# Top-k attention and two MLPs on one core: other planner costs, and PSUM accumulators moved beside the scores

## The chip, the cores and the metric

The kernel runs on one core of a Trainium2 chip. The metric is the device time of one execution in microseconds (us); lower is better. TensorE (PE) does the matmuls, VectorE (DVE), ScalarE (ACT) and GpSimd (POOL) the element-wise work, and SyncE (SP) issues nearly all DMAs.

## The reference

Three stages follow each other on 2304 tokens of width 512 (4 batches of 576 tokens, 8 heads of 64):

```python
scores = scale * np.matmul(q, k.transpose(0, 1, 3, 2))
kth = np.partition(scores, -top_k, axis=-1)[..., -top_k:-top_k + 1]
scores = np.where(scores >= kth, scores, -1000000000.0)
attn = np.exp(scores - np.max(scores, axis=-1, keepdims=True))
attn = attn / (np.sum(attn, axis=-1, keepdims=True) + 1e-09)
x = np.matmul(attn, v)                       # top_k = 32 of 576 keys
h = x @ w_in                                 # first MLP, 512 -> 2048 -> 512
x = np.where(h >= 1, h, np.where(h <= -1, 0.0, (h + 1) ** 2 / 4)) @ w_out
h = np.maximum(x @ w_in, 0.0)                # second MLP, weights of its own
out = h * h @ w_out
```

Inputs and output are float32.

## The kernel before, in words

**Tiles.** The tokens are 18 tiles `T` of 128 rows. Attention goes by slots `t = 8 * T + j`, 144 in all, one for a tile and a head. Float32 values are split into a high and a low float16 part, so that a float32 product is three float16 matmuls (`mlp_in`, line 1044, and `mlp_out`, line 1097) or comes from pairs of parts laid side by side (`scores`, line 820, and `attend`, line 900).

**One slot.** `scores` writes 128x576 scores into PSUM with four matmuls (`both<-kst,qT` in the profile). `topk_ops` (line 835) finds the 32nd largest of each row on DVE: four MAX8 (eight largest each) with three MATCH_REPLACE8 between them that blank what was found; the first MAX8 and the first MATCH_REPLACE8 read PSUM (`m<-both`, `W<-m,both`), the rest the SBUF copy `W`. POOL makes two biases `nb` from the result (line 851). ACT reads the scores again (`below`, line 862, `W<-both,nb`), takes the exponential (line 868) and writes the high part (`pc<-W`, line 876); POOL subtracts to get the low part (line 885); a DMA transposes (`pT<-pc`, line 892); and `attend` sums the 14 products with the values and a column of ones into a 65-wide accumulator in PSUM (`acc<-vst,pT`).

**One tile.** `x_part` (line 940) runs twice a tile, for four slots each: DVE reads the sums in column 64 (`rs<-acc`), takes the reciprocal, and ACT, or DVE in tiles 4 and 13 (`x<-acc,rs`), scales the four accumulators into `x`. `x` is split and transposed to `T_x`. An MLP group is 12 matmuls in (`h<-wall,T_x` or `h<-wall,T_y`), an activation on ACT and DVE (`r`), a split (`g`), a transpose (`gT<-g`) and 12 matmuls out (`o<-wall,gT`); each tile has four groups in each MLP, and the second MLP runs a tile behind the first. In the first 250 us the weights are loaded and decoded too (`wall`, line 483: ACT, POOL and DVE in turn).

**PSUM.** One tile `both` (line 818) holds two score areas, columns 0 to 575 for even slots and 960 to 1535 for odd ones. One tile `acc` (line 898) holds seven accumulators used in turn. Two tiles each are for `h` and `o`. In the built program, instructions of different engines that touch one PSUM tile wait for each other in program order, also where they touch different columns of it and where both only read.

**What sets the order.** Nothing is issued when it is called. `Book.note` (line 185) records every instruction with what it depends on and a key (`PLAN`, line 35, gives each step an offset in units of an eighth of a slot). `Book.order` (line 279) is a list scheduler: it keeps a clock for each engine, takes the engine that can start first, and there the ready instruction with the lowest key. `Book.costs` (line 251) gives each instruction a time for which its engine is busy and a time until its result can be used. `Book.emit` (line 353) issues all in the planned order, so that each engine runs its own part in order; hence nearly all instructions of the profile have the line of `emit`, 356. In this planner two engines never exclude each other: only data, buffers and the engine's own queue set a start.

Of the kernel before, what the change touches and what calls it, by code (L numbers as in the profile page):

```python
# [8 lines left out]
F32 = mybir.dt.float32  # L9
# [7 lines left out]
P = 128  # L17
# [109 lines left out]
class Room:  # L127
    def __init__(self, ring, shape, dtype, name):
        self.ring, self.shape, self.dtype, self.name = ring, shape, dtype, name
        self.writes, self.reads, self.ends, self.first, self.left, self.end, self.at = [], [], [], None, 0, 0.0, None  # L130
# [13 lines left out]
class Op:  # L144
    __slots__ = ("n", "engine", "fn", "args", "kwargs", "deps", "succ", "tiles", "new", "cost", "key", "ready", "start", "missing", "load", "move")


class Book:
# [36 lines left out]
    def note(self, engine, method, fn, args, kwargs):  # L185
# [41 lines left out]

        if method == "matmul":
            p0, p1, at = outs[0].cover()[:3]
            ends = outs[0].tile.ends  # L230
            if kwargs["start"]:
                deps.update(n for a, b, bank, n in ends if bank == at // 2048 and a < p1 and p0 < b)
            if kwargs["stop"]:
                ends[:] = [e for e in ends if e[:3] != (p0, p1, at // 2048)] + [(p0, p1, at // 2048, op.n)]
# [10 lines left out]
        op.deps = deps  # L245
        op.cost = self.costs(engine, method, args, kwargs, outs, ins)
# [4 lines left out]
    def costs(self, engine, method, args, kwargs, outs, ins):  # L251
        n = outs[0].elements() if outs else 0
        if engine == "PE":
            a = args[1].tile.dtype
            c = max(n * (4 if a is F32 else 1) / 2370.0, 0.03)
            return c, c + 0.2
        both = sum(not v.tile.ring.psum for v in ins if v.elements() > 64)
# [7 lines left out]
        if engine == "ACT" and method == "dma_start_transpose":  # L265
            return 1.35, 5.0
# [3 lines left out]
        if engine == "POOL":  # L270
            c = 0.2 + n / 490 if method == "tensor_tensor" else 0.27 + n / 1050
            return c, c + 0.06
        if method == "dma_start":
            src = args[1]
            size = 4 * (n or args[1].elements()) * 128
            return 0.5, size / 1000 / 390
        return 1.32, n * 256 / 1000 / 165

    def order(self):
# [13 lines left out]
        out = []  # L293

# [15 lines left out]
        while len(out) < len(ops):  # L310
# [16 lines left out]
            op = ops[heapq.heappop(now[e])[1]]  # L327
            op.start = t
            busy, took = op.cost
            free[e] = t + busy  # L330
            if e == "SP":
                wire = max(wire, t + 1.6) + took
                end = wire + 0.3
# [35 lines left out]
def tile_topk_attention_mlp_mlp(  # L369
# [18 lines left out]
    def rings(name, bufs, **space):  # L388
# [4 lines left out]
    ps_s, ps_a, ps_h, ps_o = (  # L393
        rings(n, m, **psum) for n, m in (("ps_s", 1), ("ps_a", 1), ("ps_h", 2), ("ps_o", 2))
    )
# [422 lines left out]
    both = ps_s.tile([P, 1536], F32, tag="s", name="both")  # L818

    def scores(t):  # L820
# [3 lines left out]
        d["s"] = ps = both[:, 960 * odd : 960 * odd + S]  # L824
# [115 lines left out]
    def x_part(T, half):  # L940
# [4 lines left out]
        runs = []  # L945
# [445 lines left out]
```

## Time and profile before

| | us |
|---|---|
| three timed executions | 1137.35, 1132.17, 1139.06 |
| median of them | 1137.35 |
| span of the profiled execution, first to last instruction | 1130.8 |
| median less that span | 6.55 |
| PE busy in it | 988.4 |
| DVE busy in it | 925.7 |
| ACT busy in it | 861.7 |
| POOL busy in it | 715.5 |

The page gives no other time for the profiled execution than its span, so what lies around the span is taken as those 6.55 us. "Busy" is the time in which at least one instruction of an engine runs. A matmul's record lasts longer than the distance to the next one, since matmuls are pipelined. A wait is shown as "engine and what it was to write <- engine and what that wrote last", with its total, the number of times, and the longest.

### The profile page before, as it was taken

The numbers are of one execution on the slowest core, as the hardware profiler recorded it, in microseconds if no ns is written. First come the engines' busy times: TensorE is split into PE (matmuls) and PEld (weight loads), VectorE is DVE, ScalarE is ACT, GpSimd is POOL, SyncE is SP. The second block draws the span as 40 slices with busy tenths as digits, with TensorE's granted clock in tenths as the row PEclk, the third lists the DMA queues.
The fourth block names the chain that finished last, engine by engine and source line by source line (L and its number), as shares of the span: only waits on it lengthen the run. The fifth ranks groups of instructions, "written<-read, shape, count | busy, mean of one in ns | idle before, by whom it ended". The sixth has DMA issues, their size and how long they took to land. (4 is left out here: it accounts for less than half of the span.)

```text
span 1130.8 us, 20675 instructions
## 1 busy us (share of the span) xinstructions
PE 988.4 (87%) x6676; PEld 479.8 (42%) x6676; DVE 925.7 (82%) x1967; ACT 861.7 (76%) x1605; POOL 715.5 (63%) x1182
## 2 busy tenths in 40 slices
PE   1267776688899999999999999999999999999997
PEld 1033333234344444444444444444444444444443
DVE  5899987798899898998989898998889998983100
ACT  4778989799768787878888777878777778776443
POOL 4696989889676755657775655567775646453221
PEclk9569887789999999999999999999999999999999
DMA  7989878667788666868877667778867676564332
GB/s 227 313 283 253 215 175 196 133 140 139 145 146 153 113 122 115 163 120 156 158 156 137 118 122 123 150 136 161 155 120 131 123 127 108 109 117 88 75 66 56
DMA packets 463389, 165.22 MB, mean 146 GB/s; under 512 B 441776, under 2 KB 448944, under 8 KB 463280
## 3 DMA queue, kind: packets, MB, share of 16 engines
q1 hardware_dynamic: 459856, 163.05, 70.2%
q10 hardware_dynamic: 3424, 0.85, 0.4%
q8 instruction: 52, 0.85, 0.3%
q14 instruction: 57, 0.47, 0.2%
HBM read 55.31 MB, written 4.72 MB: 53 GB/s over the span
## 5 line engine op out<-in xcount | busy, mean ns | idle before, releaser
L356 PE MATMUL o<-wall,gT 128*128 128x512 f16 x1728 | 420.1, 382 | 19.7 <-DMA gT<-g 19.2
L356 DVE MAX8 m<-W 128x8 f32<-128x576 f32 x432 | 326.6, 758 | 8.4
L356 POOL TENSOR_TENSOR g<-r,g 128x512 f16<-128x512 f32 x144 | 168.2, 1168 | 147.3 <-ACT g L356 124.4
L356 POOL TENSOR_TENSOR pc<-W,pc 128x64 f16<-128x64 f32 (+1 forms) x288 | 207.3, 740 | 84.2 <-ACT pc L356 65.4
L356 PEld LDWEIGHTS <-gT 128*128 128x128 f16 x1728 | 163.9, 98 | 222.8 <-DMA gT<-g 34.2
L356 PE MATMUL h<-wall,T_x 128*128 128x512 f16 x864 | 213.3, 390 | 8.5 <-DVE r L356 8.2
L356 DVE MATCH_REPLACE8 W<-m,W 128x576 f32<-128x576 f32 x288 | 213.8, 742 | 0.0
L356 PE MATMUL h<-wall,T_y 128*128 128x512 f16 x864 | 208.8, 380 | 1.3 <-DVE r L356 1.1
L356 ACT ACTIVATE W<-both,nb 128x576 f32<-128x576 f32 x144 | 106.3, 739 | 87.0 <-DVE W L356 32.5
L356 DVE MAX8 m<-both 128x8 f32<-128x576 f32 x144 | 108.9, 757 | 36.7 <-PE both L356 13.3
L356 PE MATMUL both<-kst,qT 128*128 128x64 f16 (+3 forms) x640 | 101.8, 299 | 42.0 <-ACT W L356 33.8
L356 ACT ACTIVATE W<-W,nb,esc 128x576 f32<-128x576 f32 x144 | 124.1, 862 | 6.8 <-POOL nb L356 2.7
L356 PEld LDWEIGHTS <-T_x 128*128 128x128 f16 x864 | 83.0, 100 | 102.7 <-issue 18.3
L356 PEld LDWEIGHTS <-T_y 128*128 128x128 f16 x864 | 81.5, 98 | 92.3 <-issue 2.3
L356 PEld LDWEIGHTS <-pT 128*128 128x128 f16 (+1 forms) x2240 | 92.1, 101 | 51.0 <-issue 14.2
L356 ACT ACTIVATE g<-r 128x512 f16<-128x512 f32 x144 | 90.2, 626 | 24.1 <-DVE r L356 22.7
L356 DVE MATCH_REPLACE8 W<-m,both 128x576 f32<-128x576 f32 x144 | 107.6, 748 | 0.0
L356 PE MATMUL acc<-vst,pT 128*128 128x65 f16 (+1 forms) x2240 | 100.8, 196 | 4.5 <-DMA pT<-pc 3.8
L356 ACT ACTIVATE pc<-W 128x576 f16<-128x576 f32 x144 | 97.3, 676 | 0.9
L356 ACT ACTIVATE r<-r 128x512 f32<-128x512 f32 x144 | 90.1, 626 | 1.6
L356 POOL TENSOR_SCALAR nb<-m 128x1 f32<-128x1 f32 x144 | 31.1, 216 | 87.8 <-DVE m L356 76.1
L356 ACT ACTIVATE r<-h 128x512 f32<-128x512 f32 x72 | 42.5, 591 | 49.6 <-PE h L356 46.7
(143 smaller groups left out, 1130.0 us busy)
## 6 DMA issues: line engine op xcount, KB each, us to landing
wall<-in_moe_w_in_dram SPq DMA_DIRECT2D x32, 512.0 KB, 7.1
wall<-in_moe_w_out_dram SPq DMA_DIRECT2D x30, 512.0 KB, 5.2
out_dram<-ob SPq DMA_DIRECT2D x18, 256.0 KB, 2.5
l_q<-in_q_dram SPq DMA_DIRECT2D x16, 256.0 KB, 3.4
n_v<-in_v_dram SPq DMA_DIRECT2D x24, 144.0 KB, 2.8
n_k<-in_k_dram SPq DMA_DIRECT2D x12, 288.0 KB, 3.1
l_k<-in_k_dram SPq DMA_DIRECT2D x12, 288.0 KB, 3.3
pT<-pc SPq DMA_TRANSPOSE x144, 3.3
```

Source lines behind the costliest of these rows:

```text
L356: op.fn(*(real(a) for a in op.args), **{k: real(a) for k, a in op.kwargs.items()})
```

## The change

The planner's costs are new throughout (ACT, POOL, DVE, DMA, and 0.16 us instead of 0.2 us from a matmul to its user). Three exclusions are new in `order`: an instruction isn't started while another engine still holds a PSUM tile that it touches (`held`, `apart`); POOL and a DVE instruction with two large SBUF operands exclude each other in the same way (`"port"`); and an accumulation isn't opened while another is open in the same 2 KB and half of the rows of a tile (`taken`, `shut`), which replaces the dependence through `ends`. `PLAN` stays.

The PSUM layout changes too: two tiles `s0` and `s1` of two banks each (the profile and the order name both `s`, or `s0` and `s1`). Even slots have their scores in `s0`, odd ones in `s1`; the accumulators of even slots lie in `s1` and those of odd slots in `s0`, six in each. `attend` uses accumulator `t // 2 % 6` of its side, and `x_part` reads two accumulators on each side instead of a run of up to four.

```diff
         op.deps = deps
+        op.banks = {v.tile for v in views if v.tile.ring.psum}
+        if engine == "POOL" or engine == "DVE" and sum(not v.tile.ring.psum for v in ins if v.elements() > 64) > 1:
+            op.banks.add("port")
...
         if engine == "DVE":
-            if method in ("max", "match_replace"):
-                n = 576
-            if method == "tensor_scalar" and not any(v.tile.ring.psum for v in ins + outs):
-                n *= 0.8
-            c = 0.06 + n / 960 + (0.07 if method == "match_replace" else 0.25 if both > 1 else 0.06 if method != "max" else 0)
-            return c, c + 0.03
...
+            if method == "max":
+                return 0.68, 0.75
+            if method == "match_replace":
+                return 0.76, 0.85
+            c = 0.07 + (n if method != "tensor_reduce" else 128) / 960 + (0.05 if n > 64 else 0.0)
+            return c, c + 0.08
         if engine == "ACT":
-            c = 0.17 + n / 1400 + 0.1 * sum(isinstance(kwargs.get(k), View) for k in ("bias", "scale", "accum_out"))
-            return c, c + 0.12
...
+            c = 0.155 + n / 1400 - (0.03 if wide else 0.0) + 0.09 * aps - (0.04 if n < 300 else 0.0)
+            return c, c + 0.1
...
+        held, taken, shut = {}, set(), []
+
+        def apart(op, t):
+
+            return max([t] + [end for b in op.banks for e, end in held.get(b, {}).items() if e != op.engine])
...
             op = ops[heapq.heappop(now[e])[1]]
+            if not taken.isdisjoint(op.opens):
+                shut.append(op)
+                free[e] = t
+                continue
+            later = apart(op, t)
+            if later > t:
+                heapq.heappush(soon[e], (later, op.n))
+                free[e] = t
+                continue
...
+            for b in op.banks:
+                held.setdefault(b, {})[e] = t + took + 0.08
             free[e] = t + busy
-            if e == "SP":
+            if op.load:
                 wire = max(wire, t + 1.6) + took
-                end = wire + 0.3
+                end = wire + 0.7
+            elif op.move == "dma_start_transpose":
+                wire = max(wire, t + 1.1) + took
+                end = wire + 0.4
...
-    both = ps_s.tile([P, 1536], F32, tag="s", name="both")
+    pair = tuple(ps_s.tile([P, 1024], F32, tag=f"s{i}", name=f"s{i}") for i in range(2))
+    AREA = (pair[0][:, 0:S], pair[1][:, 1024 - S : 1024])
+    ACC = tuple(pair[1 - i][:, a : a + 6 * D1].rearrange("p (i d) -> p i d", d=D1) for i, a in enumerate((0, S)))
...
-        d["s"] = ps = both[:, 960 * odd : 960 * odd + S]
+        d["s"] = ps = AREA[odd]
...
-    acc = ps_a.tile([P, 7 * D1], F32, tag="a", name="acc").rearrange("p (i d) -> p i d", d=D1)
...
-                    acc[r0 : r0 + rn, t % 7, :],
+                    ACC[odd][r0 : r0 + rn, t // 2 % 6, :],
...
-            for j, n, i in runs:
-                DVE.tensor_scalar(rs[:, j : j + n], acc[:, i : i + n, D], 1e-9, None, op0=ALU.add)
+            for a in range(2):
+                DVE.tensor_scalar(pairs[:, a], ACC[a][:, i0 : i0 + 2, D], 1e-9, None, op0=ALU.add)
```

In the built program each engine has the same instructions as before, but for DVE: 72 instead of 51 additions `rs`, and 16 instead of 12 products `x` for tiles 4 and 13. SP has 373 transposes and 235 loads or stores in both. What moves is shown at three places around slots 79 to 81. Names carry the program's buffer numbers; `m8_79` is the maxima of slot 79, `W_79` its scores, `pT_77` the transposed probabilities of slot 77. A wait names the counter of the engine or DMA queue that is waited for.

On ACT, at the second reading of slot 79's scores (`W_79` from `both` or `s1`), before:

```order
L356 ACTIVATE ob_6_7383<-o_2_6_7069,z_6_6870 128x512 [waits PE_49]
L356 ACTIVATE W_79_7268<-both_193,nb_79_7356 128x576 [waits DVE_49,PE_49,Pool_49]
L356 ACTIVATE r_66_7394<-h_66_7335,B1_705,A1_753 128x512 [waits PE_49]
L356 ACTIVATE g_65_7404<-r_65_7345 128x512 [waits DMAHW5_49,DVE_49]
L356 ACTIVATE W_79_7268<-W_79_7268,nb_79_7356,esc_9_6221 128x576 [waits Activation_49,Pool_49]
```

and now:

```order
L383 ACTIVATE h_65_7296<-h_65_7296,NG_811,A2_789 128x512
L383 ACTIVATE W_79_7277<-s1_207,nb_79_7378 128x576 [waits PE_49,Pool_49]
L383 ACTIVATE W_79_7277<-W_79_7277,nb_79_7378,esc_9_6240 128x576 [waits Activation_49,Pool_49]
L383 ACTIVATE g_65_7397<-r_65_7336 128x512 [waits DMAHW0_49,DVE_49]
L383 ACTIVATE pc_79_7402<-W_79_7277 128x576 [waits DMAHW7_49,Activation_49]
```

The wait for DVE is gone here. Over the whole program the readings of scores on ACT that wait for a DVE instruction on the same PSUM tile go from 104 to 15 of 144.

On PE, from the last matmul of slot 81's scores to slot 77's sums over the values, before:

```order
L356 LDWEIGHTS qT_10_0_7116
L356 MATMUL both_193<-kst_2_0_6114,qT_10_0_7116 128x512
L356 LDWEIGHTS pT_77_7283 [waits DMAHW3_49]
L356 MATMUL acc_476<-vst_2_5_7180,pT_77_7283 128x65 [waits Pool_49]
L356 LDWEIGHTS pT_77_7283 [waits DVE_49]
```

and now:

```order
L383 LDWEIGHTS qT_10_0_6983
L383 MATMUL s1_207<-kst_2_0_6083,qT_10_0_6983 128x512
L383 LDWEIGHTS pT_77_7298 [waits DMAHW3_49]
L383 MATMUL s0_201<-vst_2_5_6975,pT_77_7298 128x65 [waits DVE_49]
L383 LDWEIGHTS pT_77_7298
```

The first of the 14 products now waits for a DVE counter: for slot 80's first MATCH_REPLACE8, which reads the scores in the same tile. Over the whole program the sums of 79 of the 144 slots wait so for DVE's reading of scores and 31 for ACT's, from slot 48 on 53 and 26 of 96; before, none did, and 34 waited for `rs` or `x` (as 10 do now). The scores of 41 slots waited for DVE's reading of the slot just before; none does now, and 45 wait for `rs` or `x`.

On DVE, the chain of slot 79 from its first MAX8 on, before:

```order
L356 MAX m8_79_7244<-both_193 128x8 [waits PE_49,Activation_49]
L356 MAX m8_78_7149<-W_78_7174 128x8 [waits DVE_49]
L356 MATCH_REPLACE W_79_7268<-m8_79_7244,both_193 128x576 [waits DVE_49,Pool_49]
L356 TENSOR_SCALAR rs_9_7276<-acc_476 128x4 [waits PE_49]
L356 SCALAR_TENSOR_TENSOR r_64_7228<-h_64_7188,G_731,r_64_7228 128x512 [waits Activation_49]
L356 RECIPROCAL rs_9_7276<-rs_9_7276 128x4 [waits DVE_49]
L356 MAX m8_79_7244<-W_79_7268 128x8
L356 MATCH_REPLACE W_79_7268<-m8_79_7244,W_79_7268 128x576 [waits DVE_49]
```

and now:

```order
L383 MAX m8_79_7269<-s1_207 128x8 [waits PE_49,Pool_49]
L383 MATCH_REPLACE W_79_7277<-m8_79_7269,s1_207 128x576 [waits DVE_49]
L383 SCALAR_TENSOR_TENSOR r_64_7246<-h_64_7197,G_778,r_64_7246 128x512 [waits Activation_49,Pool_49]
L383 TENSOR_SCALAR rs_9_7214<-s0_201 128x2 [waits PE_49,Activation_49]
L383 MAX m8_79_7269<-W_79_7277 128x8 [waits DVE_49]
L383 RECIPROCAL rs_9_7214<-rs_9_7214 128x4 [waits DVE_49]
L383 MATCH_REPLACE W_79_7277<-m8_79_7269,W_79_7277 128x576 [waits DVE_49]
```

The other work of DVE moves to between steps of the chain that depend on each other. In the whole program a MAX8 or MATCH_REPLACE8 follows one of its own slot 425 times, 485 before. The addition `rs` now also waits for ACT: 30 of the 72 wait for ACT's reading of scores, and 18 first MAX8 wait for ACT's `x`; none of either did. By the time DVE comes to the last slot's first MAX8, the order has 15 fewer MLP matmuls ahead of it on PE: 471 of them stand behind that point, 456 before.

## Rows read from the trace of the kernel before

**Rows 1.** Windows of the run; columns in the second line.

```profile
core 0: us, PE busy (x) PEld busy (x) DVE busy (x) ACT busy (x) POOL busy (x), PEclk, DMA share, GB/s
0.00:21.00 21.00, 4.37 (x25) 2.34 (x25) 9.43 (x21) 12.37 (x25) 10.37 (x21) 1.00 0.78 250
21.00:400.00 379.00, 282.74 (x1954) 137.07 (x1954) 337.14 (x726) 303.42 (x590) 292.77 (x451) 0.86 0.80 184
400.00:1018.00 618.00, 595.60 (x4160) 292.09 (x4159) 564.61 (x1189) 493.35 (x901) 383.45 (x677) 1.00 0.72 133
1018.00:1131.00 113.00, 105.65 (x542) 48.33 (x540) 14.56 (x32) 52.60 (x92) 28.92 (x33) 1.00 0.37 71
```

**Rows 2.** TensorE's waits from 400 to 1018 us.

```profile
engine line waited for: us in total, times, longest us
PE o L356 <- DMA gT<-g: 8.3, 11, 1.6
PE h L356 <- DVE r L356: 5.3, 4, 1.8
PE both L356 <- ACT W L356: 5.2, 5, 2.0
PE both L356 <- DVE rs L356: 1.9, 1, 1.9
PE both L356 <- DVE W L356: 0.3, 1, 0.3
PE both L356 <- DVE m L356: 0.3, 1, 0.3
PE acc L356 <- DVE rs L356: 0.3, 1, 0.3
```

**Rows 3.** Tile both: first and last start, and idle time before its instructions.

```profile
L356 DVE MAX8 m<-both x144: 733/756/768, 21.0 to 1018.2; 128x8 f32<-128x576 f32 x144
...
its engine sat idle before it (us, times) until:
  ACT W L356: 62.5, 54
  DVE W L356: 37.1, 38
```

**Rows 4.** VectorE's waits from 400 to 1018 us.

```profile
DVE W L356 <- ACT W L356: 13.7, 20, 1.0
DVE m L356 <- ACT W L356: 7.6, 8, 1.1
DVE m L356 <- PE both L356: 3.6, 8, 1.1
```

**Rows 5.** ScalarE's waits from 400 to 1018 us.

```profile
ACT W L356 <- DVE W L356: 28.4, 30, 2.3
...
ACT W L356 <- DVE rs L356: 6.1, 9, 1.4
ACT W L356 <- DVE m L356: 6.0, 9, 1.1
```

**Rows 6.** VectorE's waits from 21 to 400 us.

```profile
DVE m L356 <- PE both L356: 9.7, 8, 2.4
DVE W L356 <- ACT W L356: 5.3, 7, 0.9
...
DVE m L356 <- ACT W L356: 0.9, 1, 0.9
```

**Rows 7.** VectorE in order of time: start us, us, instruction.

```profile
599.54 0.76 DVE L356 MAX8 m<-W 128x8 f32<-128x576 f32 x1
600.34 0.09 DVE L356 MATCH_VALUE_LOAD W<-m,W 128x8 f32 x1
600.41 0.74 DVE L356 MATCH_REPLACE8 W<-m,W 128x576 f32<-128x576 f32 x1
601.08 0.76 DVE L356 MAX8 m<-both 128x8 f32<-128x576 f32 x1
601.75 0.74 DVE L356 MAX8 m<-W 128x8 f32<-128x576 f32 x1
...
604.71 0.09 DVE L356 MATCH_VALUE_LOAD W<-m,W 128x8 f32 x1
...
605.56 0.76 DVE L356 MAX8 m<-W 128x8 f32<-128x576 f32 x1
```

**Rows 8.** Groups of VectorE from 400 to 1018 us: count, busy us, mean ns, idle before.

```profile
L356 DVE SCALAR_TENSOR_TENSOR r<-h,G,r 128x512 f32<-128x512 f32 x48 | 35.4, 737 | 1.0 <-POOL z L356 0.6 <-POOL nb L356 0.4
...
L356 DVE TENSOR_SCALAR rs<-acc 128x4 f32<-128x4 f32 (+3 forms) x33 | 4.8, 146 | 1.5 <-PE acc L356 1.4
...
L356 DVE TENSOR_TENSOR x<-acc,rs 64x64 f32<-64x64 f32 (+2 forms) x6 | 2.0, 331 | 0.1
```

**Rows 9.** Chain that ended last: start us, us, piece.

```profile
1019.67 2.59 PE h L356 x12
```

**Rows 10.** A group of VectorE from 0 to 250 us, columns as in rows 8.

```profile
L356 DVE SCALAR_TENSOR_TENSOR wall<-wall 128x512 int32<-128x512 int32 x62 | 54.0, 880 | 8.9 <-POOL wall L356 4.1 <-POOL esc L356 2.6 <-ACT wall L356 1.1
```

More of the change, by code (lines that the diff above doesn't have):

```diff
@@ L144 @@
 class Op:
-    __slots__ = ("n", "engine", "fn", "args", "kwargs", "deps", "succ", "tiles", "new", "cost", "key", "ready", "start", "missing", "load", "move")
+    __slots__ = ("n", "engine", "fn", "args", "kwargs", "deps", "succ", "tiles", "new", "cost", "key", "ready", "start", "missing", "load", "move", "banks", "opens", "closes")
 class Book:
@@ L226, in note @@
             t.writes.append((c, op.n))
+        op.opens = op.closes = []
         if method == "matmul":
             p0, p1, at = outs[0].cover()[:3]
[L230 to L234, printed above, removed]
+            parts = [(outs[0].tile, at // 2048, p) for p in range(p0 // 64, (p1 + 63) // 64)]
+            op.opens = parts if kwargs["start"] else []
+            op.closes = parts if kwargs["stop"] else []
         op.load = method == "dma_start"
@@ L251, in costs @@
     def costs(self, engine, method, args, kwargs, outs, ins):
-        n = outs[0].elements() if outs else 0
+        views = [v for v in outs + ins if v.elements() > 8]
+        n = max((v.elements() for v in outs), default=0)
+        wide = any(v.tile.ring.psum for v in views)
+        aps = sum(isinstance(a, View) and a.elements() == 1 for a in (*args[2:], kwargs.get("bias"), kwargs.get("scale"), kwargs.get("accum_out")))
         if engine == "PE":
-            a = args[1].tile.dtype
-            c = max(n * (4 if a is F32 else 1) / 2370.0, 0.03)
-            return c, c + 0.2
@@ L267, in costs @@
-        if engine == "ACT":
-            c = 0.17 + n / 1400 + 0.1 * sum(isinstance(kwargs.get(k), View) for k in ("bias", "scale", "accum_out"))
-            return c, c + 0.12
[L270 to L277, printed above, removed]
+            c = max(n * (4 if args[2].ap.dtype is F32 else 1) / 2370.0, 0.03)
@@ L944, in x_part @@
         rs = rs_[T]
-        runs = []
-        for j in js:
-            if (8 * T + j) % 7 and runs:
-                runs[-1][1] += 1
-            else:
-                runs.append([j, 1, (8 * T + j) % 7])
+        pairs = rs.rearrange("p (j a) -> p a j", a=2)[:, :, 2 * half : 2 * half + 2]
+        i0 = (4 * T + 2 * half) % 6
         def add():
-            for j, n, i in runs:
-                DVE.tensor_scalar(rs[:, j : j + n], acc[:, i : i + n, D], 1e-9, None, op0=ALU.add)
+            for a in range(2):
+                DVE.tensor_scalar(pairs[:, a], ACC[a][:, i0 : i0 + 2, D], 1e-9, None, op0=ALU.add)
         def reciprocal():
@@ L967, in scale @@
             if T in (4, 13):
-                to = x[64 * half : 64 * half + 64].rearrange("p (j a) d -> p a j d", a=2)
-                for j, n, i in runs:
+                to = x[64 * half : 64 * half + 64].rearrange("p (j b a) d -> p a b j d", a=2, b=2)
+                for b in range(2):
                     for a in range(2):
@@ L978, in scale @@
             else:
-                for j in js:
-                    ACT.activation(x[:, j], acc[:, (8 * T + j) % 7, 0:D], AF.Copy, scale=rs[:, j : j + 1])
+                for j in sorted(js, key=lambda j: j % 2):
+                    ACT.activation(x[:, j], ACC[j % 2][:, i0 + j // 2 % 2, 0:D], AF.Copy, scale=rs[:, j : j + 1])
         return [add, reciprocal, scale] + (token_trans(lambda: ld["x", T], xT, T, "xT", f"x{T}") if half else [])
```

30 lines of the change are left out of this document (20 added, 10 removed).

## The prediction, made before the changed kernel had run

> **What bounds the kernel now.** I read the windows first [rows 1], by four stages. Up to 21 us nothing of attention runs. From 21 to 400 us weights are decoded beside the first 48 slots: DVE is busy for 337.14 of 379 us, PE for 282.74, at a granted clock of 0.86. From 400 to 1018 us PE is busy for 595.60 of 618 us and DVE for 564.61; behind 1018 us DVE has almost nothing (14.56 of 113) and PE works off MLP groups (105.65). So the time is the time at which the last slot is reached plus a tail of matmuls, and in the middle stage PE can give back at most 618 - 595.60 = 22.4 us, however much is saved elsewhere. This cap decides the size of everything below.
>
> PE's waits of that stage came second [rows 2]. Of the 22.4 us, 8.3 are for the transposed `gT` and 5.3 for DVE's `r`, both inside the MLP's own chain; 5.2 + 1.9 + 0.3 + 0.3 = 7.7 us stand before scores, and the accumulators cost 0.3. Third came the tile that both score areas share [rows 3]: first MAX8 from 21.0 to 1018.2 us, and 62.5 us of engines' idle time before its users ended by ACT's `W` and 37.1 by DVE's, summed over engines. Then I took the same waits by engine. In the middle stage DVE waits 13.7 + 7.6 = 21.3 us for ACT's `W` before it may touch `both` [rows 4], which for one slot's own chain makes no sense, since ACT's reading there belongs to another slot: it is the shared tile. In the other direction ACT waits 28.4 + 6.1 + 6.0 = 40.5 us for DVE before its `W` [rows 5], but ACT is busy for only 493.35 of 618 us [rows 1] and has room. From 21 to 400 us DVE's waits around scores are 9.7 us for PE's `both` and 5.3 + 0.9 = 6.2 us for ACT's `W` [rows 6].
>
> **The change, part by part.**
>
> *Two score tiles.* DVE's reading of one slot no longer excludes ACT's reading of the one before. In the order 28 first MATCH_REPLACE8 and 14 first MAX8 of DVE wait for ACT's reading of the slot before; none does now, so 21.3 + 6.2 = 27.5 us of DVE's idle time lose their cause. ACT's 40.5 us lose theirs in most places (104 such waits become 15); what they bring is an earlier `W`, which PE's scores wait for.
>
> *Accumulators beside the scores.* New are 30 `rs` additions that wait for ACT's reading and 18 first MAX8 that wait for ACT's `x`. Queued behind them on DVE is the next slot's chain. A wait of this kind that showed in the middle stage took 21.3 us / (20 + 8) = 0.76 us [rows 4]. Bounds: 0, if all are late enough, and 48 x 0.76 = 36 us. I take a quarter, 9 us, since the planner now keeps these apart by itself and so puts other work first. On PE the sums over the values wait for DVE in 53 and for ACT in 26 of the last 96 slots; behind them stand MLP matmuls, and behind those ACT's `r`. The trace of before has no such wait (0.3 us in all before `acc`). Bounds: 0, and one DVE instruction each, 53 x 0.75 = 40 us [rows 7]. I take what the scores' waits lose, so PE's 7.7 us are swapped, not saved, as the nearest rows are those.
>
> *DVE's order and count.* The 21 more `rs` are 0.146 us each, 3.1 us, and the four more `x` pieces at most 4 x 0.331 = 1.3 us [rows 8]. Against this stands the chain. A step that depends on the one before starts 600.34 - 599.54 = 0.80 us after a MAX8 and 605.56 - 604.71 = 0.85 us after the value load of a MATCH_REPLACE8; an independent one starts 601.75 - 601.08 = 0.67 us after a MAX8 [rows 7]. With 60 fewer dependent neighbours (425 for 485) DVE saves 60 x 0.13 = 7.8 us. Net about -3.4 us on DVE.
>
> *The new costs.* By the old costs (with the 0.03 us that the planner adds to a user on the same engine) a dependent MAX8 and MATCH_REPLACE8 took 0.72 + 0.79 = 1.51 us of the plan, by the new 0.78 + 0.88 = 1.66, and the trace shows 0.80 + 0.85 = 1.65 [rows 7]. So the old plan let DVE run some 9% too fast, and the places where PE and ACT meet it were planned too early; the new plan meets it where it is. What this is worth is not in any row. Above it can't exceed PE's 13.6 us for `gT` and `r` in the middle stage [rows 2]; below, a plan with the same list and other ties may lose as much. I count it in the half taken next.
>
> *Sum.* DVE can gain 27.5 - 9 + 3.4 = 22 us on its way to the last slot, about 17 of it in the middle stage. There PE's cap is 22.4 us, of which the swapped 7.7 are not for sale, and 13.6 us are the MLP's. PE moves on only as far as these shrink; I take half the cap, 11 us. From 21 to 400 us, where PE has slack, I take half of DVE's 6.2 us, 3 us. Together -14 us. The 15 MLP matmuls that now stand behind the last slot cost nothing in all, as PE does them either way: at 2.59 / 12 = 0.216 us [rows 9] they make the tail 3.2 us longer and let the last slot come that much sooner. SP has the same transposes and loads; their landing is in the `gT` waits counted above. ACT's and POOL's work is the same. So the span goes from 1130.8 to 1116.8 us, and with the 6.55 us by which the median stands above the span, to 1123.4 us.
>
> **Two rules of the Trainium skill.** The trace shows that sharing a tile costs [rows 3, 4]. The Trainium skill, PSUM — Partial Sum Buffer, section on bank collisions, says that two engines on one bank, in the same quarter of the partitions, must be kept apart by the program, readers included, while different banks are free. By that rule the accumulators, alone in a bank before, now share one with the last 64 columns of a score area, which speaks against this change; the program waits for whole tiles, wider than the rule. It would give the third rival's sum. Next, a decode on DVE takes 0.880 us with both operands in SBUF [rows 10] and an instruction of the same size with one in PSUM 0.737 [rows 8]. The Trainium skill, SBUF — State Buffer, section on who interferes with whom, says that such a DVE instruction and a POOL instruction hold one port in turn and the later one blocks. By that rule, with which these rows agree, planning them apart moves the blocking and could save DVE 62 x 0.143 = 8.9 us at best, which lies on the side of the first rival.
>
> **Rivals.**
>
> *First, more than half.* If the early stage also runs by the better plan, DVE's 9.7 + 5.3 + 0.9 = 15.9 us there [rows 6] go, and the whole 22.4 us of the middle stage: -38.3 us, 1099 us. For it speaks that all of PE's idle time there hangs on DVE or on what follows DVE. Against it: `gT` waits are a DMA's, and the early stage also waits for decodes.
>
> *Second, nothing.* PE's 13.6 us are the MLP's own distance from `r` to `gT`, which no layout of scores touches, and 7.7 us are swapped for waits before the sums. DVE then only waits elsewhere, in front of scores that PE delivers at its own pace. The time stays at 1137 us. For it speaks PE's 96% in the middle stage [rows 1]; against it, that PE waits for `r` at all.
>
> *Third, slower: the sums over the values.* In the order shown they follow straight behind a slot's scores and wait for a MATCH_REPLACE8 of DVE. If DVE is one instruction behind plan at every second of the 53, PE stands still 27 x 0.75 = 20 us with MLP matmuls behind it; less the 7.7 us that go, this is +12.3 us: 1143.1 + 6.55 = 1149.7 us. It decides once these waits exceed 7.7 us plus what else is gained, about 22 us in all for a loss against the forecast's 14. For it speaks that both engines have almost no slack; against it, that the new costs fit DVE to 1%.
>
> **How the numbers follow.** The forecast has 0.45, its own range 1115 to 1132 us (a gain of 5 to 22); the first rival 0.15, the second 0.22, the third 0.18. A measurement of this kernel can tell about 1%, that is below 1126 and above 1149 us. Of the forecast 0.33 lies below 1126 and 0.12 above; with the first rival this makes 0.48 faster. Same is 0.12 + 0.22 and 0.02 of the third, 0.36; slower 0.16. The range goes from the first rival's 1099 to the third's 1150, with a microsecond more at either end: 1098 to 1151 us.
>
> **What would show it.** Right: DVE's waits for ACT's `W` before `both` in the middle stage fall from 21.3 us to under 10; the last slot's first MAX8 starts at about 1001 us instead of 1018.2 (14 + 3.2 sooner); PE's idle time between slot 48 and the last falls by a third to two thirds; the tail behind the last slot is some 116 us. Wrong: PE's waits before the sums over 15 us (third rival), or PE's idle time in the middle unchanged with `gT` and `r` as before (second). If the early stage alone is shorter by over 10 us, the step that failed is the one that takes half of 6.2 us there.

## The result, and the profile after

| | before | after |
|---|---|---|
| median of the timed runs, us | 1136.79 (4 runs) | 1122.78 (4 runs: 1121.18 to 1124.46) |
| ratio after / before | | 0.9898 (95%: 0.9874 to 0.9922) |
| span of the profiled execution, us | 1130.8 | 1120.4 |
| first MAX8 of slot 48, us | 404.8 | 401.6 |
| first MAX8 of the last slot, us | 1018.2 | 1005.6 |
| between these two, us | 613.4 | 604.0 |
| from there to the end, us | 112.6 | 114.8 |

The kernel became 1.0% faster by the ratio, some 11.6 us (8.9 to 14.3 by its interval); the two medians of four stand 14.0 us apart, and 1123.4 us was forecast. Between the two profiled executions the difference is only 1130.8 - 1120.4 = 10.4 us. Here after's profiled execution has a time of its own, 1122.30 us, so 1.9 us lie around its span. In 62 later executions of before, taken beside the experiments, the time stands 1.7 to 1.9 us above the span as well. So before's profiled execution took some 1132.7 us and was one of the faster ones: most of the 6.55 us that the prediction carried over as "around the span" was a difference between executions. The sum was 14 for a measured 10.4 between the spans, and the median was met so closely by luck.

The granted clock doesn't explain the gain. Of those 62 executions of before, the 24 with a mean granted clock under 0.952 have a median of 1136.8 us, and the 13 at 0.970 or more one of 1135.1; after's four stand at 0.969 to 0.977.

The windows of after, to be read against [rows 1]:

```profile
core 0: us, PE busy (x) PEld busy (x) DVE busy (x) ACT busy (x) POOL busy (x), PEclk, DMA share, GB/s
...
21.00:400.00 379.00, 282.43 (x1966) 138.62 (x1967) 331.89 (x742) 307.17 (x598) 296.04 (x455) 0.94 0.79 184
...
400.00:1018.00 618.00, 605.68 (x4240) 295.62 (x4238) 569.83 (x1212) 506.80 (x914) 388.06 (x683) 1.00 0.74 135
1018.00:1121.00 103.00, 95.56 (x457) 42.49 (x454) 7.75 (x19) 41.96 (x72) 23.34 (x25) 0.98 0.33 66
```

From 400 to 1018 us PE is busy for 605.68 us instead of 595.60, so 12.3 us of idle time are left of 22.4, with the same clock. ScalarE's and VectorE's busy times rise as well: the three do more in the same stretch. From 21 to 400 us PE's busy time is the same, though the granted clock is another, 0.94 for 0.86.

PE's waits of the same stage, against [rows 2]:

```profile
PE o L383 <- DMA gT<-g: 9.0, 14, 1.5
PE o L383 <- DVE r L383: 1.0, 1, 1.0
PE s L383 <- ACT x L383: 0.6, 1, 0.6
PE s L383 <- POOL vst L383: 0.6, 1, 0.6
PE h L383 <- DMA T_x<-hl_x: 0.3, 1, 0.3
PE s L383 <- ACT W L383: 0.2, 1, 0.2
PE s L383 <- DVE x L383: 0.2, 1, 0.2
```

`h` no longer waits for `r` (5.3 us before), though `o` does once (1.0); the 9.0 us for the transposed `gT` (8.3 before) are what stays. Scores and sums now both write a tile named `s`; the groups tell them apart (count, busy us, mean ns, idle before and what ended it):

```profile
L383 PE MATMUL s<-kst,qT 128*128 128x64 f16 (+3 forms) x416 | 63.4, 287 | 0.6 <-ACT x L383 0.6
L383 PE MATMUL s<-vst,pT 128*128 128x65 f16 (+1 forms) x1484 | 63.3, 194 | 1.0 <-POOL vst L383 0.6 <-ACT W L383 0.2 <-DVE x L383 0.2
```

The 7.7 us before scores have become 0.6. The sums over the values, with 0.3 us before, have 1.0, and no wait for a MATCH_REPLACE8 of DVE among them, though the sums of 53 slots have that wait in their program.

The tile of the scores and accumulators, against [rows 3] (first and last start, and idle time before its users on all engines):

```profile
L383 DVE MAX8 m<-s x144: 725/766/768, 23.7 to 1005.6; 128x8 f32<-128x576 f32 x144
...
its engine sat idle before it (us, times) until:
  PE s L383: 47.1, 55
  POOL nb L383: 45.1, 47
```

ACT's and DVE's `W`, 62.5 and 37.1 us before, are no longer the two first (ACT's `W` still has 34.6); PE's writes of `s` and POOL's `nb` are, which is mostly the slot's own chain. The same by engine, DVE first, against [rows 4]:

```profile
DVE m L383 <- PE s L383: 11.8, 24, 1.5
DVE m L383 <- POOL nb L383: 5.0, 10, 1.3
...
DVE rs L383 <- ACT W L383: 1.0, 2, 0.8
```

DVE's waits for ACT's `W` before scores (21.3 us) are gone, and only 1.0 us came for the new wait of `rs`. But DVE's waits for PE's scores went from 3.6 to 11.8 us, and 5.0 us have come for `nb`: part of what DVE gained it now spends waiting for PE. ACT, against [rows 5], has lost nearly all of its 40.5 us (1.8 are left) and waits more for PE's `h` (22.0 us before) and for `nb` (13.7 before):

```profile
ACT r L383 <- PE h L383: 50.3, 55, 2.4
ACT W L383 <- POOL nb L383: 17.8, 27, 1.9
```

### The profile page after: what moved, and what is told of

Its sections match the earlier page's. It is cut to its first block, busy times and chain, and to the rows that moved or that the text cites. A ratio compares the mean times of both kernels' runs of the same rounds, so it can differ in the third digit from the quotient of the medians.

```text
span 1120.4 us, 20689 instructions
## 1 busy us (share of the span) xinstructions
PE 986.2 (88%) x6676; PEld 478.3 (43%) x6676; DVE 918.2 (82%) x1992; ACT 868.2 (77%) x1605; POOL 719.0 (64%) x1182
## 4 chain that ended last, share of the span: by engine, by line
PE 31%; POOL 15%; issue 10%; ACT 9%; DMA 9%; DVE 9%; SPq 1%; POOLq 0%; ACTq 0%; DVEq 0%
PE o L383 14%; PE h L383 12%; DMA gT<-g 5%; POOL pc L383 4%; DVE m L383 4%; PE s L383 4%; DVE W L383 3%; POOL g L383 3%; POOL wall L383 3%; ACT r L383 2%; ACT W L383 2%; POOL nb L383 2%; SPq L383 1%; DMA l_q<-in_q_dram 1%; ACT g L383 1%
## 5 line engine op out<-in xcount | busy, mean ns | idle before, releaser
L383 PE MATMUL o<-wall,gT 128*128 128x512 f16 x1728 | 427.7, 383 | 18.6 <-DMA gT<-g 17.1
L383 PE MATMUL h<-wall,T_x 128*128 128x512 f16 x864 | 209.7, 384 | 1.7 <-DVE r L383 1.1
L383 ACT ACTIVATE W<-s,nb 128x576 f32<-128x576 f32 x144 | 106.0, 736 | 46.4 <-POOL nb L383 39.8
L383 DVE MAX8 m<-s 128x8 f32<-128x576 f32 x144 | 109.5, 760 | 37.9 <-PE s L383 25.8
L383 PE MATMUL s<-kst,qT 128*128 128x64 f16 (+3 forms) x640 | 102.0, 300 | 35.9 <-ACT W L383 33.0
L383 PE MATMUL s<-vst,pT 128*128 128x65 f16 (+1 forms) x2240 | 98.9, 196 | 13.9 <-DMA pT<-pc 9.5
L383 DVE MATCH_REPLACE8 W<-m,s 128x576 f32<-128x576 f32 x144 | 107.6, 748 | 0.0
L383 ACT ACTIVATE r<-h,B,A 128x512 f32<-128x512 f32 x72 | 55.8, 775 | 42.1 <-PE h L383 41.3
```

Source lines behind the costliest of these rows:

```text
L383: op.fn(*(real(a) for a in op.args), **{k: real(a) for k, a in op.kwargs.items()})
```

## The experiments

The change has three parts that can be set apart: the layout (L), the exclusions in the planner (E) and the costs with the landing times of DMAs (C). Together with before and after, six kernels make all eight combinations. For every run the table gives the ratio to before with its interval, and from the profiled execution the time of slot 48's and of the last slot's first MAX8 and the distance between them. Runs with a single execution have no interval.

| run | parts | ratio (95%) | slot 48, us | last slot, us | between, us |
|---|---|---|---|---|---|
| before | none | 1 | 404.8 | 1018.2 | 613.4 |
| e1 | L | 1.0195 (1.0163 to 1.0228) | 409.1 | 1039.2 | 630.1 |
| e12 | E | 1.0109 (1.0086 to 1.0133) | 408.8 | 1033.6 | 624.8 |
| e6 | C | 1.0213 (1.0189 to 1.0238) | 400.9 | 1042.0 | 641.1 |
| e4 | L, E | 1.0019 (0.9998 to 1.0040) | 404.9 | 1019.9 | 615.0 |
| e3 | L, C | 1.0118 (1.0084 to 1.0152) | 405.6 | 1029.7 | 624.1 |
| e2 | E, C | 0.9930 (0.9909 to 0.9952) | 404.1 | 1009.8 | 605.7 |
| after | L, E, C | 0.9898 (0.9874 to 0.9922) | 401.6 | 1005.6 | 604.0 |
| e5 | after without the port | 0.9897 (0.9873 to 0.9922) | 400.1 | 1007.6 | 607.5 |
| e9 | L, E, DVE's costs alone | 0.9919 (0.9899 to 0.9939) | 408.4 | 1009.5 | 601.1 |
| e13 | after, one cost + 0.01 us | 0.9944 (0.9924 to 0.9964) | 408.3 | 1010.3 | 602.0 |
| e10 | after, MLP a slot earlier | 1.0012 (0.9998 to 1.0026) | 413.5 | 1028.8 | 615.3 |
| e7 | after, a third less MLP on PE | one execution, 1080.21 us | 406.3 | 1001.0 | 594.7 |
| e8 | after, one MAX8 pair less | one execution, 1145.68 us | 399.8 | 1030.6 | 630.8 |

### The layout alone

```diff
-    both = ps_s.tile([P, 1536], F32, tag="s", name="both")
+    pair = tuple(ps_s.tile([P, 1024], F32, tag=f"s{i}", name=f"s{i}") for i in range(2))
...
-                    acc[r0 : r0 + rn, t % 7, :],
+                    ACC[odd][r0 : r0 + rn, t // 2 % 6, :],
```

(on the kernel before, with `AREA` and `x_part` as in the change)

> Only the PSUM layout is new (two score tiles, accumulators beside them); costs and planner are those of before. Theory (layout and planner share the gain): DVE's waits for ACT's W before score tiles vanish (21.3 us from 400 to 1018 us before, under 5 here), but the plan doesn't know of the new waits before the sums over the values, and PE stands 5 to 15 us for DVE there; 1125 to 1135 us, about 1130. Rival A (the costs alone do it): within 3 us of before, about 1137. Rival B (the layout alone does it): 1120 to 1125. If the sums' waits are as dear as the prediction's third rival: over 1145.

It was slower by 2.0%. PE's groups of scores and sums from 400 to 1018 us, then DVE's wait from 400 to 1000 us:

```profile
L356 PE MATMUL s<-vst,pT 128*128 128x65 f16 (+1 forms) x1400 | 63.8, 194 | 22.7 <-ACT W L356 12.2 <-DMA pT<-pc 4.0 <-DVE rs L356 2.4
L356 PE MATMUL s<-kst,qT 128*128 128x512 f16 (+3 forms) x401 | 62.2, 287 | 3.9 <-ACT W L356 2.4 <-ACT x L356 1.2
```

```profile
DVE m L356 <- PE s L356: 31.3, 33, 5.6
```

Here the third rival's mechanism shows: PE stands idle for 22.7 us before the sums (0.3 before), where the rival had 20, with the MLP's matmuls behind. It waits mostly for ACT's reading of scores, 12.2 us, and not for DVE's, as the rival and the expectation had it; 4.0 us end with the transposed `pT` and not with the shared tile. Scores have only 3.9 us of their own, but they stand in the same queue, and DVE waits 31.3 us for them (3.6 before). The 27.5 us of DVE's waits that the prediction had as the largest gain are more than paid back; of those for ACT's `W` one of 6.0 us is left, where under 5 was expected. The expected place is right; the time, 1156.00 us, is far above the theory's range and is what was expected for sums as dear as in the third rival, over 1145.

### The planner alone

After's planner, with the tiles `both` and `acc` of before:

```diff
-    pair = tuple(ps_s.tile([P, 1024], F32, tag=f"s{i}", name=f"s{i}") for i in range(2))
+    both = ps_s.tile([P, 1536], F32, tag="s", name="both")
...
-                    ACC[odd][r0 : r0 + rn, t // 2 % 6, :],
+                    acc[r0 : r0 + rn, t % 7, :],
```

> New costs and exclusions in the planner, the PSUM layout of before (one tile both, seven accumulators of their own). Theory: the planner's half of the gain, 1127 to 1133 us; DVE's waits for ACT's W before both shrink but don't vanish, since the tile still excludes them, only now by plan. Rival A (costs alone): 1121 to 1125, as after. Rival B (layout alone): about 1137.

PE's and DVE's waits from 400 to 1000 us (in total, times, longest):

```profile
PE o L383 <- DMA gT<-g: 13.3, 16, 1.4
PE h L383 <- DVE gsa_k L383: 0.2, 1, 0.2
```

```profile
DVE m L383 <- PE both L383: 19.4, 26, 1.5
DVE W L383 <- ACT W L383: 4.6, 12, 1.0
```

0.9930: most of the gain, with the shared tile still there (1126.72 us, just below the theory's range). All of PE's waits over 0.2 us are for `gT`. DVE's waits for ACT's `W` shrink to 4.6 us, while those for scores grow to 19.4 (3.6 before). With exact costs, then, the tile's exclusion costs little where the plan contains it; the same costs and layout without the exclusions (e6 below) give 1.0213.

### Exclusions or costs left out

Without the exclusions on PSUM tiles and on the port (the one on open accumulations stays; costs and layout are after's):

```diff
-            later = apart(op, t)
+            later = t
```

> As after, but the planner doesn't keep two engines apart on a PSUM tile, nor POOL and DVE on the port (the line that delays an instruction is taken out); costs and layout are after's. Theory: the instructions stand where they must wait unplanned, PE waits over 5 us before the sums over the values from 400 us on (0 to 1 in after), 1126 to 1132 us. Rival A (costs alone): 1121 to 1125.

PE's groups of scores and sums from 400 to 1018 us, and DVE's wait for scores from 400 to 1000 us:

```profile
L383 PE MATMUL s<-kst,qT 128*128 128x512 f16 (+3 forms) x408 | 61.9, 287 | 1.5 <-DVE x L383 1.0 <-ACT W L383 0.5
L383 PE MATMUL s<-vst,pT 128*128 128x65 f16 (+1 forms) x1428 | 60.7, 194 | 11.8 <-ACT W L383 11.8
```

```profile
DVE m L383 <- PE s L383: 24.5, 32, 3.0
```

Slower than before by 1.2%, worse than expected. PE waits 11.8 us before the sums, over the expected 5, all for ACT's reading of scores (0.2 in after), and DVE waits 24.5 us for scores behind them (11.8 in after, to 1018 us). That the accumulators lie beside the scores costs PE this much where the plan doesn't see it, and 1.0 us where it does.

With the costs of before (exclusions and layout of after):

```diff
-            if method == "max":
-                return 0.68, 0.75
...
+            c = 0.06 + n / 960 + (0.07 if method == "match_replace" else 0.25 if both > 1 else 0.06 if method != "max" else 0)
+            return c, c + 0.03
```

> As after, but with the costs of before (and its landing times of DMAs); exclusions and layout are after's. Theory: the plan lets DVE run some 9% too fast, so PE's matmuls meet DVE too early: PE's idle time from 400 us to the last slot is 18 us or more (12 in after), 1127 to 1133 us. Rival A (costs alone do it): about 1137. Rival B (layout alone): 1120 to 1125.

1.0019, so nothing is left of the gain. The window's row:

```profile
400.00:1018.00 618.00, 601.90 (x4167) 294.17 (x4166) 568.70 (x1210) 493.25 (x902) 385.84 (x679) 0.99 0.77 134
```

The time, 1136.37 us, is above the theory's range and at rival A's (the costs alone do it), which the next run excludes. PE is idle for 618 - 601.90 = 16.1 us, under the 18 expected and only 3.8 more than in after, while the stage from slot 48 to the last is 11.0 us longer. Of the rest some 24 x 0.216 = 5.2 us are 24 MLP matmuls that after does before slot 48 and this order behind it. So what old costs lose is for the most part not the waiting of PE for a late DVE that the theory had. With the costs alone (no exclusions, old layout; the diff is the reverse of this one on the kernel before):

> The kernel before, with the new costs and landing times alone: no exclusion, the old layout. Theory after the first four runs (neither half of the planner is worth anything alone, since exact costs without the tile's exclusions pack engines against waits that the plan doesn't see): 1134 to 1148 us. Rival (the costs are an improvement of their own): 1124 to 1131 us.

PE's and DVE's waits from 400 to 1000 us:

```profile
PE o L359 <- DMA gT<-g: 23.1, 28, 2.4
PE both L359 <- ACT W L359: 5.1, 6, 1.6
```

```profile
DVE W L359 <- ACT W L359: 25.3, 35, 1.1
DVE m L359 <- PE both L359: 22.5, 20, 4.3
```

It is the slowest of the eight combinations, and above the range of the theory. DVE waits 25.3 us for ACT's `W`, twice as long as before: that is the tile's exclusion, which this plan doesn't contain. But PE waits no longer for ACT's `W` than before (5.1 for 5.2 us); its largest wait is for the transposed `gT`, 23.1 us (7.4 before in the same stretch), so the theory's reason is shown for DVE alone. And the exclusions alone (old costs, old layout):

> The planner's exclusions alone: the costs and the PSUM layout of before. With after, before and the runs so far this completes the eight combinations of layout, exclusions and costs. Theory (exclusions need exact costs, which is why old costs with exclusions and the new layout gave nothing): 1131 to 1142 us. Rival (exclusions are worth their gain alone, and costs only matter through the layout): 1123 to 1130 us.

1.0109, above the range of the theory too; that neither half stands alone was right, that it costs nothing was not. All three parts lose by themselves; costs and exclusions together win. On the new layout each of the two takes something back from e1's 1.0195 (the exclusions to 1.0019, the costs to 1.0118), but only both together come below 1.

### Which costs

After with the costs of before, but DVE's new ones kept:

```diff
+            if method == "max":
+                return 0.68, 0.75
+            if method == "match_replace":
+                return 0.76, 0.85
+            c = 0.07 + (n if method != "tensor_reduce" else 128) / 960 + (0.05 if n > 64 else 0.0)
+            return c, c + 0.08
```

(the other branches as before)

> As after, with the costs of before for all but DVE, whose new costs stay. Theory (the step of the prediction that the old plan let DVE run 9% too fast is the one that the costs are worth): at least two thirds of the 13.6 us between old costs and new come back, 1122 to 1128 us. Rival (ACT's, POOL's and the DMAs' costs matter as much): 1129 to 1137 us.

From old costs, 1.0019, to all new ones, 0.9898, are 1.2%; DVE's alone bring 1.0%, to 0.9919. The stage from slot 48 to the last is 601.1 us, as good as after's. So DVE's costs, which the prediction found 9% too low for a dependent pair, carry most of what the costs are worth, within the scatter that the last section of the experiments shows. By which wait they do is open, as e4's idle time of PE says.

### The port

```diff
-            op.banks.add("port")
+            pass
```

> As after, but the plan doesn't keep POOL and DVE apart on the port; the exclusion on PSUM tiles stays. Theory (the PSUM exclusion and the costs carry the gain): within 4 us of after, 1120 to 1127 us. Rival (the port carries a share of it, by the decodes of the first 400 us): slot 48 is reached 4 us later or more, 1128 us or more.

The ratio is after's. What the port in the plan does is seen in the decodes of the weights (VectorE's group from 0 to 250 us: count, busy us, mean ns, idle before), first in after, then without it, then in e13 below, whose plan keeps the two apart like after's, against [rows 10]:

```profile
L383 DVE SCALAR_TENSOR_TENSOR wall<-wall 128x512 int32<-128x512 int32 x62 | 49.6, 800 | 16.7 <-POOL wall L383 9.1 <-ACT wall L383 5.5 <-POOL esc L383 1.6
```

```profile
L383 DVE SCALAR_TENSOR_TENSOR wall<-wall 128x512 int32<-128x512 int32 x62 | 53.3, 860 | 18.3 <-POOL wall L383 12.0 <-issue 4.1 <-POOL nb L383 1.1
```

```profile
L383 DVE SCALAR_TENSOR_TENSOR wall<-wall 128x512 int32<-128x512 int32 x62 | 56.8, 916 | 13.1 <-POOL wall L383 6.2 <-ACT wall L383 4.4 <-POOL esc L383 1.5
```

In after a decode takes 0.800 us and without the port in the plan 0.860 (0.880 before), 62 x 0.06 = 3.7 us less of DVE. That this comes of the port isn't shown: in the nine runs whose plan keeps the two apart (after, e2, e4, e7 to e10, e12, e13) the mean lies between 0.800 and 0.916 us, in the five others between 0.823 and 0.880, so each order gives it another value. Nor does it buy time: the idle time before the decodes is 16.7 us with the port and 18.3 without, 8.9 before, and slot 48 comes at 401.6 us with it and at 400.1 without. The Trainium skill, SBUF — State Buffer, section on who interferes with whom, calls the ports that VectorE and GpSimd share an exclusive lock. Single decodes of after last between 0.660 and 1.480 us, which fits that, but the 8.9 us that the prediction estimated by it were not to be had.

### Which engine sets the pace

After without the product of the activations' low part, PE having 249 us less to do:

```diff
-        PE.matmul(h, src[:, 0, fb, :], w_lo(w, c, 0, 512), start=False, stop=False)
-        PE.matmul(h, src[:, 1, fb, :], w_hi(w, c, 0, 512), start=False, stop=(fb == 3))
+        PE.matmul(h, src[:, 0, fb, :], w_lo(w, c, 0, 512), start=False, stop=(fb == 3))
```

(and the same in `mlp_out`)

> As after, but each MLP matmul triple is a pair: the product of the low part of the activations is left out, in both MLPs, so PE has 1152 matmuls less (1152 x 0.216 = 249 us). Theory (PE paces the stage from slot 48 to the last, DVE is next): from slot 48 to the last slot 604.0 us become 570 to 588, as DVE has some 28 us of waits there to give back and no more; the tail falls from 115 to about 80 us; 1050 to 1075 us in all. Rival (DVE paces that stage already): 598 to 606 us for it, and 1080 to 1092 in all.

The window's row, and PE's and DVE's waits, from 400 to 1000 us:

```profile
400.00:1000.00 600.00, 486.96 (x3451) 229.43 (x3449) 548.24 (x1212) 495.25 (x920) 386.53 (x680) 0.94 0.76 139
```

```profile
PE s L383 <- ACT W L383: 31.2, 25, 4.6
PE o L383 <- DMA gT<-g: 23.1, 27, 3.4
PE h L383 <- DVE r L383: 19.6, 15, 3.5
```

```profile
DVE rs L383 <- PE s L383: 15.9, 11, 3.0
DVE m L383 <- PE s L383: 14.3, 23, 1.9
```

1080.21 us: of the 249 us only 42 come out, nearly all of them behind the last slot. From slot 48 to the last it is 594.7 us, 9.3 less than after, between the theory's range and the rival's; the total is the rival's. With a third of the MLP gone PE is idle for 600 - 486.96 = 113 us, and the slots hardly come faster: in this order at least, something other than the amount of PE's work keeps them within 10 us of after's time. PE's waits point to the slot's own chain (ACT's `W`, the transposes, DVE). PE also runs a little slower than in after, at a granted clock of 0.94 instead of 1.00 (a matmul of `o` takes 396 ns from slot 48 to the last instead of 379), so the run may understate what less work gives. In the other direction, 238 us less DVE work; the kernel then keeps 24 keys of a row instead of 32:

```diff
-TOPK = 32
+TOPK = 24
...
-        st[t]["ops"][7]()
+        st[t]["ops"][-1]()
...
-    ORDERS = (tuple(((0, i),) for i in range(7)) + ((),), (((0, 0),), ((1, 4),), ((0, 1),), ((1, 5),), ((0, 2),), ((1, 6),), ((0, 3),), ()))
+    ORDERS = (tuple(((0, i),) for i in range(5)) + ((),) * 3, (((0, 0),), ((1, 4),), ((0, 1),), ((1, 5),), ((0, 2),), ((1, 6),), ((0, 3),), ()))
```

> As after, but DVE finds the 24th largest score instead of the 32nd: one MAX8 and one MATCH_REPLACE8 fewer in each slot, 144 x 1.65 = 238 us less DVE work. Theory (PE and DVE pace the stage from slot 48 to the last together, PE's floor close under the time): 604.0 us for that stage become 588 to 598, as PE has 12 us of idle time there; slot 48 comes 20 to 50 us sooner, as DVE is the busiest there; 1060 to 1095 us in all. Rival (DVE alone paces it, PE only follows): the stage loses over 60 us.

Slower than after, by 23 us. The windows' row from 400 to 1000 us (columns as above) and the waits of PE and DVE there:

```profile
400.00:1000.00 600.00, 573.30 (x3924) 277.66 (x3923) 400.93 (x872) 457.79 (x857) 364.43 (x644) 0.99 0.72 131
```

```profile
PE o L383 <- DMA gT<-g: 17.0, 20, 3.2
PE s L383 <- ACT W L383: 3.6, 4, 2.0
```

```profile
DVE m L383 <- PE s L383: 135.6, 58, 6.4
```

DVE has 135.6 us of waiting for scores, so it doesn't set the pace; PE is busy for 573.30 of 600 us, less than in after (587.68 in the same stretch), with 17.0 us for `gT`. The list scheduler drew another order for the lighter DVE, and that order is worse for PE. From slot 48 to the last, 26.8 us longer than in after, PE is idle for 26.7 us instead of 12.3 and busy for 604.1 instead of 591.7, at a granted clock of 0.99 and with 24 MLP matmuls (5.2 us) more in that stage. Why the scheduler draws such an order stays open. Neither of the two expectations held. As far as one order of each goes, lightening PE alone gives this stage 9 us (at the lower clock) and lightening DVE alone nothing.

### How far orders scatter

After with 0.17 instead of 0.16 us from a matmul to its user:

```diff
-            return c, c + 0.16
+            return c, c + 0.17
```

> As after, with one cost moved by 0.01 us: 0.17 instead of 0.16 us from a matmul to its user. The trace can't tell the two apart (a matmul's record lasts 379 ns at a pitch of 216, a difference of 163), but the greedy plan answers with another order of thousands of rows. Theory (the gain belongs to exact costs and exclusions together, and an order drawn with them is good whichever way ties fall): within 5 us of after, 1118 to 1128 us. Rival (orders of this planner scatter by more than the gain, and after is a lucky one): 1130 us or more.

0.9944: half of the gain. By the medians, 1128.38 us lies just outside the 5 us of the theory and short of the rival's 1130. The windows show where:

```profile
0.00:400.00 400.00, 279.54 (x1941) 137.45 (x1942) 338.45 (x748) 313.52 (x611) 303.77 (x470) 0.91 0.78 186
400.00:1000.00 600.00, 589.25 (x4126) 287.52 (x4125) 559.08 (x1194) 494.91 (x893) 379.73 (x670) 1.00 0.74 136
```

From 400 to 1000 us PE is busy for 589.25 us (587.68 in after), and from slot 48 to the last it takes 602.0 us, 2 less than after. All of the loss lies before: slot 48 comes at 408.3 us, 6.7 us later. Last, after with the MLP's groups a slot earlier (`N0=11`), as the one attempt at something better:

```diff
-    sp_i2=120, sp_o2=190, spch=(0, 0, 1), spd_i1=8, spd_o1=8, spd_i2=8, spd_o2=8, mc0=55, N0=12, early=0,
+    sp_i2=120, sp_o2=190, spch=(0, 0, 1), spd_i1=8, spd_o1=8, spd_i2=8, spd_o2=8, mc0=55, N0=11, early=0,
```

> As after, with the MLP's groups planned one slot earlier (N0 11 instead of 12). Theory (PE is full from slot 48 on, but idle for a quarter of the first 400 us, so work that moves there shortens the tail): one group of 24 matmuls, 24 x 0.216 = 5.2 us, moves; 1116 to 1121 us. Rival (MLP work in the first 400 us slows the slots as much, since ACT and DVE do part of it): 1121 to 1126 us.

1.0012, against both expectations: slot 48 comes 12 us later, and the stage behind it takes 615.3 us. So exact costs and exclusions with one entry of `PLAN` changed give nothing at all.

Two things no run tests: how far orders of before's planner scatter, and whether `PLAN`, which all other runs share, suits one planner better than another. Part of what the half changes lose may be that. The size of the gain, 1.0%, is the size for these two orders.

## Why the prediction was right, step by step

The time, the sign and the size of the gain were right, and so was the cap that set the size; the part of the change to which the sum gave them was not, and several terms agreed by luck.

- *PE's cap in the middle stage, half of it taken (11 us).* Right in size: 22.4 us of PE's idle time became 12.3, and from slot 48 to the last the kernel gained 613.4 - 604.0 = 9.4 us. Five orders drawn with exclusions and exact DVE costs, `PLAN` untouched (after, e2, e5, e9, e13), lie between 601.1 and 607.5 us there; the six without one of the two, between 613.4 and 641.1. Three of the six (e4, e6, e12) do 24 MLP matmuls, 5.2 us, in this stage that the others do before it; less these, the six lie between 609.8 and 635.9. This part of the gain is shown to come from the two together, as far as single orders can show it.
- *Two score tiles: 27.5 us of DVE's waits.* The waits did go, and the step failed as the source of the gain. With the layout alone the kernel lost 2.0%, with the planner alone it had 0.7% of the 1.0%. DVE's idle time before scores turned into waits for PE (3.6 to 11.8 us). Whether the layout adds anything to the planner isn't settled: after and e2 differ by 0.3%, less than after and e13.
- *The new costs, "in no row, counted in the half".* This was the term that carries the sum, and only together with the exclusions, which the prediction left without a term of their own. DVE's costs bring 1.0 of the 1.2% between e4 and after. That they do it because PE no longer meets DVE too early isn't shown: PE's idle time differs by only 3.8 us between e4 and after.
- *DVE's order and count, 3.4 us less.* DVE's busy time fell from 925.7 to 918.2 us. Of these 7.5 us, 4.4 are the decodes (54.0 to 49.6), which the term didn't count, so 3.1 us are left for it.
- *PE's 7.7 us are swapped, not saved.* Wrong: they went (0.6 us is left before scores), and the sums came only to 1.0 us from 0.3, together 6.4 us gained. The sum had the half come out of the MLP's 13.6 us; of these 10.0 stayed (9.0 for `gT`, 1.0 for `r`), 3.6 us gained. So the half is made of other waits than was said, and that the size agreed is luck in this respect.
- *The new waits of `rs` and of the first MAX8, a quarter, 9 us.* Oversized: 1.0 us for `rs` in the middle stage, and none for `x` among its waits over 0.3 us.
- *From 21 to 400 us: half of 6.2 us, 3 us.* The measured 404.8 - 401.6 = 3.2 us agrees, but no cause is shown. DVE's waits there moved instead of shrinking (columns as in rows 6):

```profile
DVE m L383 <- PE s L383: 13.9, 11, 5.4
DVE rs L383 <- PE s L383: 8.2, 8, 2.3
DVE wall L383 <- POOL wall L383: 7.6, 11, 1.2
DVE wall L383 <- ACT wall L383: 5.5, 3, 2.9
```

13.9 us for scores (9.7 before), and 8.2 for the sums. In all the orders tried with `PLAN` as it was, slot 48 comes between 399.8 and 409.1 us, before's 404.8 in their midst. So the agreement of the two numbers can't be told from chance.

- *The tail and the last slot.* 112.6 became 114.8 us, for a forecast of 3.2 us more, but not by the 15 matmuls. In the traces 478 MLP matmuls start behind the last slot's first MAX8, 476 before, so the 15 of the order hardly show in time. What grew are the matmuls of `o`: 387 ns each there instead of 379, 252 x 0.008 = 2.0 us, at a granted clock of 0.98 from 1018 us on (1.00 before). The last slot came at 1005.6 us, where about 1001 was forecast.
- *First rival, more than half.* It didn't come: 12.3 of PE's 22.4 us stayed, and the early stage gave 3.2 of 15.9.
- *Third rival.* Its mechanism is real, 22.7 us in e1 and 11.8 in e3, and after escapes it because its plan contains it; what PE then waits for is ACT's reading rather than DVE's. The rule on PSUM banks of the Trainium skill (PSUM — Partial Sum Buffer, section on bank collisions), which was set beside it, asks that two engines be kept apart on one bank. The 22.7 us of e1 fit that. But the rule spoke for the change as much as against it: a bank is half of a 1024-wide tile, 512 columns, so before, the columns 512 to 575 of the even score area and 960 to 1023 of the odd one lay in one bank too, and every reading takes all 576 columns of its area. So these runs can't tell waits for a bank from waits for a whole tile. No run here has the accumulators in a bank of their own beside two score tiles, so what their place alone costs isn't shown.
- *Second rival, nothing.* Its argument, that the MLP's own waits stay, holds for `gT` and not for `r`.

## What to carry to other kernels

Before trusting an order that a planner draws, compare its costs with starts in a trace (here 1.51 us planned for a dependent pair that takes 1.65) and ask which waits the program has that the planner doesn't model; correct one without the other and the kernel may get slower, as three half changes did by 1 to 2%. When one engine is busy for 96% of a stage (PE here) and another for 91% (DVE), a wait that goes on the second can come back as a wait for the first (DVE's for scores, 3.6 to 11.8 us), so bound the gain by the idle time of the fuller one. And when an order is drawn greedily, shift a cost within its uncertainty and measure again before crediting any part with less than half a per cent.

## What was not expected of the hardware and the order

The scatter: 0.01 us in one cost moved the time by 0.46% of before's and slot 48 by 6.7 us. The lighter DVE: 238 us less of its work made the kernel 23 us slower. And a decode on DVE took 0.800 us in one order and 0.916 in another whose plan keeps POOL and DVE apart just the same. The granted clock from 21 to 400 us rose from 0.86 to 0.94, while PE's busy time there stayed at 282 us; at 0.94 (after, e3, e5, e12) slot 48 comes between 400.1 and 408.8 us, before's 404.8 among them, so it shows no effect on the slots.
